# Retention and two gated layers on one core: one shared GpSimd/VectorE port in the planner, held slots for partial sums, a later sine table, and one raw weight buffer for each stream

## The chip, the cores and the metric

One core of one Trainium2 chip. The metric is device time of one execution in microseconds (us), median of several runs. Engines by the profile's names: PE (TensorE, matmul), PEld (its weight loads), DVE (VectorE), ACT (ScalarE), POOL (GpSimd), SP (SyncE, which issues the DMAs here).

## The reference

```python
# retention, per head h (B=2, H=8, S=768, D=64), float32
state = gamma * state + outer(k[t], v[t]);   y[t] = scale * q[t] @ state
x = y as (1536 tokens, 512)
# first layer pair: weights (512, 2048) and (2048, 512)
h = x @ w1_in;  x = (h * tanh(softplus(h))) @ w1_out
# second layer pair, same shapes
h = x @ w2_in;  out = (h * cos(h)) @ w2_out
```

q, k, v are float32, the four weight matrices are drawn as 64-bit floats and reach the chip as raw bits (pairs of 32-bit words).

## The kernel before, in words

**Stages.** The retention runs first (to about 44 us). Then come eight groups `gi = 4 m + G`: m is the layer pair (0 mish, 1 cosine), G one of four column groups of 512 of the 2048 inner features. Tokens lie in three blocks j of 512. A product in float32 is three matmuls of rounded halves (`TERMS`: high x high, high x low, low x high).

**First layer of a group.** For group 0 all three blocks go by `gemm1` (L552). From group 1 on, blocks 0 and 1 are done together by a scheme that needs seven products where eight would do the plain way, `wino` (L510), in two half passes p = 0, 1 of `mini` (L883). A half pass is one product of six matmuls after the other on PE: p1, p2, p6, a fill, p5, a fill, c12, p7, a fill, p4. A *fill* is one unit of second-layer work, six matmuls of `gemm2` (L580), taken from an iterator `before` with `take`. Between the products, partial sums move: ACT copies bank d to the tile U (`wino_copy`, L518) after p1, p6 and p5, and DVE adds U to a bank (`wino_add`, L521), called c11, c22 and c21. p6, p5 and c12 write the bank that a copy has just read, so each waits for its copy; p4 accumulates on the bank that c22 writes, so p4 waits for c22. Block 2 goes by `gemm1` between half passes. After each block and half, ACT takes the activation (mish, L587, or the cosine in several steps from L601), rounds it to g (L630), and DVE makes the low part of g (L634); the second layer then uses it.

**Second layer.** Eight `gemm2` units for each block of a group, in bank pairs; DVE adds the result to `acc` (`out_add`, L650).

**Weights.** A tile of weights is `(which, gi, u)`: "i" or "o" (first or second layer), u = 0, 1 one half of the group's. SP loads it in two DMAs of 512 KB (`w_load`, L240) into a raw buffer. Both streams share one ring of two raw buffers (`raw_p`, L211). DVE turns the bits into float32: `w_abs` L252, `w_clamp` L258, `w_exponent` L262, `w_sign` L268, `w_low` L289. ACT rounds the high part (L283), POOL makes the low part (L297). For "i" tiles POOL and ACT also build T, the sums and differences that the seven-product scheme needs (L306, L312, L316, L320, L324); T's raw sums lie in the raw buffer, so that of an "i" tile is held until T is done.

**What sets the order.** The program is written down as operations of a `Plan` (L86): each has an engine, a cost in us, what it needs and which buffers it uses. `order` (L139) is a list scheduler over these costs. PE's operations keep the order in which they are written; for DVE, ACT, POOL and SP the planner picks what is ready first, then what has the longest tail. In before, a shared DVE operation (`SHARED`) that would start in a POOL operation waits for its end, and the other way round, but each looks only at the last operation of the other side. The instructions are then issued in that order, and each engine runs its own in that order.

**Places that the prediction speaks of.** The first half pass, of group 1, follows 13 fill units (8 of `tiles_out(0,0,0)`, 5 by `take(before, AHEAD[0])`). The half pass of group 4 is the first of the cosine layer: `at["sin"]` is an ACT operation (L590) that loads ACT's table for the sine and may run once the last mish is done.

```python
take(before, AHEAD[0])                 # AHEAD = (5, 5)
for gi in range(1, 2 * NG):
    mini(m, G, 0, lambda: take(before, 1))
    g_split()
    take(before, AHEAD[1] if G else 3)
```

Of the kernel before, what the change touches and what calls it, by code (L numbers as in the profile page):

```python
# [61 lines left out]
AHEAD = (5, 5)  # L62

# [22 lines left out]
class Plan:  # L86
# [5 lines left out]
    AHEAD = 1000  # L92
# [11 lines left out]
    def op(self, engine, cost, fn, *args, needs=(), uses=(), new=None):  # L104
        n = len(self.ops)
        uses = list(uses)
        before = set(needs)
        reuse = []
        for key, bufs, *tag in [] if new is None else new if isinstance(new, list) else [new]:
            line = self.lines.setdefault(tag[0] if tag else key[0], [])  # L110
            if line:
                before.add(self.owner[line[-1]])
            if len(line) >= bufs:
                reuse.append(line[-bufs])
            line.append(key)
# [10 lines left out]
        self.ops.append(dict(engine=engine, cost=cost, fn=fn, args=args, before=before, reuse=reuse, att=att))  # L126
        return n

    def wait(self, n, after):
        first, then = self.ops[n]["engine"], self.ops[after]["engine"]  # L130
        if first == then or first is None:
            return 0.0
        return self.LANDING if first == "SP" else self.WIRE
# [5 lines left out]
    def order(self):  # L139
# [21 lines left out]
        pool = shared = (0.0, 0.0)  # L161
        self.start, self.end, order = {}, {}, []
        while ready:
            first = {}
# [7 lines left out]
            for e in first.keys() & {"DVE", "ACT"}:  # L172
                t, _, n = first[e]
                for k, at in ready.items():
                    at = max(at, free[e])
                    if ops[k]["engine"] == e and at < t + ops[n]["cost"] and tail[k] > tail[first[e][2]] + self.AHEAD:
                        first[e] = (at, -tail[k], k)
            t, _, n = min(first.values())
            o = ops[n]
            e = o["engine"]  # L180
            if self.shares(n):
                shared = (t, t + o["cost"])
            if e == "POOL":
                t = shared[1] if shared[0] <= t < shared[1] else t
                pool = (t, t + o["cost"])
# [18 lines left out]
def retention_two_mlps(ctx: ExitStack, tc: tile.TileContext, qkv, w1i, w1o, w2i, w2o, consts, out):  # L204
# [6 lines left out]
    raw_p = ctx.enter_context(tc.tile_pool(name="raw", bufs=2))  # L211
# [19 lines left out]

    def w_load(it, ns):
        which, gi, u = it
        m, G = divmod(gi, NG)
        src = (wins if which == "i" else wouts)[m]
        if it not in raw_t:
            raw_t[it] = raw_p.tile([128, 2, 512, 2], U32, tag="raw", name="raw")
# [90 lines left out]
    att = {}  # L328
# [347 lines left out]
    def weight(it, between=lambda: None):  # L676
        raw, mag, w = ("raw", it), ("mag", it), ("w", it)
        first, single = it == ("i", 0, 0), it[:2] in (("i", 0), ("o", 0))
        if single:
            loads = [op("SP", 1.25, w_load, it, (0,), new=(raw, 2))]  # L680
            between()
            loads.append(op("SP", 1.25, w_load, it, (1,), uses=[raw]))
        else:
            loads = [op("SP", 2.5, w_load, it, (0, 1), new=(raw, 2))]
        for load, ns in zip(loads, [slice(0, 1), slice(1, 2)] if single else [slice(0, 2)]):
# [5 lines left out]
            elif first:  # L691
                at["act", it, ns.start] = last = op("ACT", 0.62, w_abs_act, it, ns.start, needs=[load], new=new, uses=[raw, mag])
            else:
                at["act", it, ns.start] = last = op("DVE", 0.75 * c, w_abs, it, ns, needs=[load], new=new, uses=[raw, mag])
            at["clamp", it, ns.start] = last = op("DVE", 0.75 * c, w_clamp, it, ns, needs=[last], uses=[mag])
            at["exponent", it, ns.start] = last = op("DVE", 0.75 * c, w_exponent, it, ns, needs=[last], uses=[mag])
            last = op("DVE", 1.27 * c, w_sign, it, ns, needs=[last], uses=[mag, raw])
# [4 lines left out]
            def low_op(needs):  # L702
                at["dve low", it, ns.start] = n = op("DVE", 1.27 * c, w_low, it, ns, single, needs=needs, uses=[mag, raw])
                return n

            def high_op(needs):
                at["high", it, ns.start] = n = op("ACT", 1.08 * c, w_high_part, it, ns, needs=needs, uses=[mag, w])
# [10 lines left out]
            for n in range(ns.start, ns.stop):  # L718
                at["w", it, n] = op(
                    *(("DVE", 0.72) if on_dve else ("POOL", 1.25)), w_low_part, it, slice(n, n + 1), on_dve,  # L720
                    needs=[high, low], uses=[w, raw if single else mag],
                )
        if it[0] == "i" and it[1]:
            t = ("T", it)
            last = op("POOL", 1.1, w_first_differences, it, needs=[low], uses=[raw, mag])
            last = op("POOL", 0.75, w_second_sum, it, needs=[last], uses=[raw, mag])
            last = op("POOL", 0.75, w_last_difference, it, needs=[last], uses=[raw, mag])
            last = op("ACT", 1.06, w_t_high, it, needs=[last, at["ret"]], new=(t, 1, "T"), uses=[raw])
            for part in (slice(0, 2), slice(2, 4)):
                at["T", it] = op("POOL", 1.25, w_t_low, it, part, needs=[last], uses=[raw, t])  # L730
# [103 lines left out]
    def tile_in(m, G, j, f, parts=range(KD), only=None):  # L834
# [16 lines left out]
        if m == 0:  # L851
            at["g"].append((k, [op("ACT", 1.06, mish, k, needs=[last, at["table"]], uses=hs)], hs))
# [3 lines left out]
    def cosine(unit, needs, hs):  # L856
# [3 lines left out]
        last = op("ACT", 0.58 * n, cos_whole, unit, needs=needs + [at["angle"], at["sin"]], new=[(a, 1, t) for t in lines], uses=hs)  # L860
        last = op("DVE", 0.64 * n, cos_angle, unit, needs=[last], uses=[a] + hs)
        last = op("ACT", 0.58 * n, cos_size, unit, needs=[last], uses=[a])
        last = op("ACT", 0.58 * n, cos_clamp, unit, needs=[last], uses=[a])
        last = op("ACT", 0.58 * n, cos_sin, unit, needs=[last], uses=[a])
        return op("DVE", 0.64 * n, g_mul, unit, needs=[last], uses=[a] + hs)

    def g_split():

        while at["g"] and free_g:
# [4 lines left out]
            if len(needs) > 1:  # L874
                at["g", k] = []
                for f in range(2):
                    high = op("ACT", 0.62, half_high, k, f, needs=[needs[f]], new=None if f else new, uses=[g, uses[f]])
                    at["g", k].append(op("DVE", 0.72, half_low, k, f, needs=[high], uses=[g, uses[f]]))
                continue
            last = op("ACT", 1.06, g_high, k, needs=needs, new=new, uses=uses)  # L880
            at["g", k] = [op("DVE", 1.35, g_low, k, needs=[last], uses=[g] + uses)]

    def mini(m, G, p, fill):  # L883
# [31 lines left out]
        for j, (needs, hs) in enumerate((([c11, c12], [b["c"], b["d"]]), ([c21, c22], [b["b"], b["a"]]))):  # L915
            k = (gi, j, p)
            if m == 0:
                at["g"].append((k, [op("ACT", 1.06, mish, k, needs=needs + [at["table"]], uses=hs)], hs))
# [5 lines left out]
    def tile_out(m, G, j, d, u, cols=slice(0, DM)):  # L924
# [17 lines left out]
        if G == 0:  # L942
            last = op("ACT", 1.05, out_first, m, G, j, p, needs=[last, at["close"]], uses=os + [acc], new=None if p else (acc, NJ))
        else:
            last = op("DVE", 1.25, out_add, m, G, j, p, needs=[last] + prior, uses=os + [acc])
        at["acc", m, j, p] = [last]
        if m == 0 and G == NG - 1:
            x = ("x", 1, j)
            if (j, p) != (1, 0):
                high = op("ACT", 1.05, x2_high, j, p, needs=[last], uses=[acc, x], new=None if x in plan.owner else (x, 1, "x%d" % j))  # L950
                at.setdefault(x, []).append(op("DVE", 1.27, x2_low, j, p, needs=[high], uses=[acc, x]))
# [161 lines left out]
    def sums(m, needs, done):  # L1113
# [9 lines left out]
        def sum_of(to, a, b, plus, *after):  # L1123
            return op("DVE", 1.27, s_op, m, to, a, b, plus, needs=[new, *after], uses=uses)
# [5 lines left out]
        for n, last in ((3, s3), (2, s2), (1, s1), (4, s4)):  # L1130
            more = uses + ([("x", m, 1)] if n == 4 else [])
            high = op("ACT", 1.05, s_high, m, n, needs=[last, *(done if n == 4 else [])], uses=more)
            at["S", m, n] = [op("DVE", 1.27, s_low, m, n, needs=[high], uses=more)]
        return s1, s2, s3, s4

    read = sums(0, [at["ret"]], j1_done)
# [17 lines left out]
    take(before, AHEAD[0])  # L1154
    for gi in range(1, 2 * NG):
# [4 lines left out]
        take(before, AHEAD[1] if G else 3)  # L1160
# [74 lines left out]
```

## Time and profile before

| what | us |
| --- | --- |
| median of 3 runs (lowest, highest) | 558.77 (556.99, 558.89) |
| profiled execution, its own time | 560.37 |
| its span | 558.3 |
| PE busy | 547.9 (98%) |
| DVE, ACT, POOL busy | 393.2, 314.0, 189.6 |
| mean granted TensorE clock | 0.994 of full speed |

The profile is of one execution, 1.60 us above the median of the runs. Its time is 2.07 us longer than its span. PE is busy nearly all the time, so the rows to read are those that tell when PE waited.

### The profile page before, as it was taken

How to read it: one execution, taken by the hardware profiler on the slowest of the kernel's cores; microseconds unless marked ns; L12 is line 12 of the kernel's file. 1: busy time of each engine (PE TensorE's matmuls, PEld its weight loads, DVE VectorE, ACT ScalarE, POOL GpSimd, SP SyncE). 2: the span in 40 equal slices, each digit the busy share in tenths (PEclk: the TensorE clock that was granted, in tenths of full speed). 3: DMA queues.
4: the chain of work that ended last, by engine and by line, in shares of the span. 5: the costliest groups of instructions: out<-in, count | busy, mean ns of one | idle time of the engine just before them, and what ended most of it. 6: DMA issues, size and time to landing. Idle time of an engine off the chain costs nothing.

```text
span 558.3 us, 7458 instructions
## 1 busy us (share of the span) xinstructions
PE 547.9 (98%) x2968; PEld 455.2 (82%) x2968; DVE 393.2 (70%) x449; ACT 314.0 (56%) x417; POOL 189.6 (34%) x166
## 2 busy tenths in 40 slices
PE   8999999899999999999999999999999999999997
PEld 6898888688888888888877888888888888888886
DVE  5689896877365586457787798659849696768452
ACT  4374453444233314333185997899586867786360
POOL 6670007436341155114422317332541146131000
PEclk9899999999999999999998999999999999999999
DMA  8982310250222210222201220131201222020103
GB/s 290 411 328 101 127 75 1 76 209 18 75 77 75 77 56 20 75 77 76 76 0 62 89 76 15 66 146 76 77 0 77 75 76 75 1 76 1 75 22 130
DMA packets 16162, 49.33 MB, mean 88 GB/s; under 512 B 1792, under 2 KB 2176, under 8 KB 16128
## 3 DMA queue, kind: packets, MB, share of 16 engines
q1 hardware_dynamic: 16128, 48.86, 23.5%
q8 instruction: 23, 0.38, 0.3%
q14 instruction: 11, 0.09, 0.0%
HBM read 45.71 MB, written 3.15 MB: 87 GB/s over the span
## 4 chain that ended last, share of the span: by engine, by line
PE 94%; DMA 2%; DVE 1%; ACT 1%; issue 1%; POOL 0%; SPq 0%; DVEq 0%
PE bank L580 46%; PE bank L510 23%; PE bank L552 20%; DMA qkv<-qkv_dram 2%; PE bank L436 2%; PE bank L397 1%; PE bank L446 1%; PE bank L411 1%; DVE mag L262 0%; DVE bank L521 0%; POOL raw L306 0%; ACT L590 0%; DVE mag L289 0%; DVE mag L268 0%; DVE mag L258 0%
## 5 line engine op out<-in xcount | busy, mean ns | idle before, releaser
L580 PE MATMUL bank<-g,wo 128*128 128x512 f32 x576 | 137.2, 392 | 0.0
L580 PE MATMUL bank<-wo,g 128*128 128x512 f32 (+2 forms) x588 | 136.1, 385 | 0.0
L580 PEld LDWEIGHTS bank<-g,wo 128*128 128x128 f32 x576 | 109.0, 189 | 22.8
L580 PEld LDWEIGHTS bank<-wo,g 128*128 128x128 f32 x588 | 109.1, 188 | 22.4 <-POOL wo L297 0.4
L552 PE MATMUL bank<-x,wi 128*128 128x512 f32 x480 | 110.2, 389 | 0.0
L552 PEld LDWEIGHTS bank<-x,wi 128*128 128x128 f32 x480 | 90.0, 188 | 18.8 <-issue 0.2
L324 POOL TENSOR_TENSOR T<-raw,T 128x512 fp32r<-128x512 f32 x28 | 39.0, 1412 | 92.3 <-ACT T L320 78.7
L297 POOL TENSOR_TENSOR wo<-mag,wo 128x512 fp32r<-128x512 f32 x28 | 36.6, 1328 | 93.9 <-ACT wo L283 82.5
L634 DVE TENSOR_TENSOR g<-bank,g 128x1024 fp32r<-128x1024 f32 x40 | 48.8, 1221 | 26.8 <-ACT g L630 26.7
L510 PE MATMUL bank<-S,T 128*128 128x512 f32 x252 | 64.8, 392 | 2.4 <-ACT U L518 2.4
L510 PE MATMUL bank<-x,wi 128*128 128x512 f32 x252 | 61.8, 389 | 0.0
L650 DVE TENSOR_TENSOR acc<-bank,acc 128x1024 f32<-128x1024 f32 x35 | 42.8, 1222 | 25.6 <-PE bank L580 25.2
L510 PEld LDWEIGHTS bank<-S,T 128*128 128x128 f32 x252 | 47.4, 189 | 13.1 <-ACT U L518 3.3
L521 DVE TENSOR_TENSOR bank<-bank,U 128x512 f32<-128x512 f32 x42 | 29.3, 697 | 38.1 <-PE bank L510 37.2
L623 DVE TENSOR_TENSOR bank<-angle,bank 128x512 f32<-128x512 f32 (+1 forms) x32 | 30.6, 959 | 36.0 <-ACT angle L619 35.8
L510 PEld LDWEIGHTS bank<-x,wi 128*128 128x128 f32 x252 | 47.2, 188 | 10.0 <-ACT U L518 0.2
L587 ACT ACTIVATE bank<-bank 128x1024 f32<-128x1024 f32 x24 | 24.2, 1009 | 53.1 <-PE bank L552 37.3
L518 ACT COPY U<-bank 128x512 f32<-128x512 f32 x42 | 24.6, 586 | 50.5 <-PE bank L510 50.0
L297 POOL TENSOR_TENSOR wi<-mag,wi 128x512 fp32r<-128x512 f32 x28 | 40.4, 1464 | 33.3 <-ACT wi L283 33.3
L306 POOL TENSOR_TENSOR raw<-mag 128x512 f32<-128x512 f32 x14 | 19.2, 1372 | 91.8 <-DVE mag L289 62.5
L630 ACT CAST g<-bank 128x1024 fp32r<-128x1024 f32 x40 | 40.7, 1017 | 8.5 <-DVE bank L623 5.2
L268 DVE SCALAR_TENSOR_TENSOR mag<-raw,mag 128x1024 uint32<-128x1024 uint32 (+1 forms) x36 | 43.0, 1196 | 0.6
(82 smaller groups left out, 628.6 us busy)
## 6 DMA issues: line engine op xcount, KB each, us to landing
raw<-w1i_dram SPq DMA_DIRECT2D x16, 512.0 KB, 4.0
raw<-w1o_dram SPq DMA_DIRECT2D x16, 512.0 KB, 4.0
raw<-w2i_dram SPq DMA_DIRECT2D x16, 512.0 KB, 3.6
raw<-w2o_dram SPq DMA_DIRECT2D x16, 512.0 KB, 3.7
qkv<-qkv_dram SPq DMA_DIRECT2D x12, 512.0 KB, 7.4
qkv<-qkv_dram SPq DMA_DIRECT2D x22, 256.0 KB, 6.9
out_dram<-acc SPq DMA_DIRECT2D x11, 256.0 KB, 2.0
out_dram<-acc SPq DMA_DIRECT2D x1, 160.0 KB, 1.7
```

The costliest lines, as they stand in the source:

```text
L268: nc.vector.scalar_tensor_tensor(out=a, in0=high, scalar=0xC0000000, in1=a, op0=ALU.bitwise_and, op1=ALU.bitwise_or)
L297: eng.tensor_sub(out=w[:, :, 1], in0=w_all_of(it, single)[:, ns].bitcast(F32), in1=w[:, :, 0].bitcast(F32))
L324: nc.gpsimd.tensor_sub(out=t[:, :, 1], in0=t_of(it)[:, part], in1=t[:, :, 0].bitcast(F32))
L510: nc.tensor.matmul(ps, lhs, rhs, start=(not more and kk + i == 0), stop=(kk == 1 and i == last), skip_group_check=True)
L518: nc.scalar.copy(out=copies[0][:, n], in_=bank[:, WINO_BANK["d"], :])
L521: nc.vector.tensor_add(out=bank[:, WINO_BANK[to], :], in0=bank[:, WINO_BANK[of], :], in1=copies[0][:, n])
L552: nc.tensor.matmul(h, w[:, f % 2, a, kk * 128 : (kk + 1) * 128], x[:, b, kk, :], start=(a + b + kk == 0), stop=(a == 1 and kk == KD - 1),)
L580: nc.tensor.matmul(ps, lhs, rhs, start=(n == 0), stop=(n == 3 * GF - 1))
L623: nc.vector.tensor_mul(out=h, in0=a, in1=h)
L630: nc.scalar.copy(out=g_t[k][:, :, 0, :], in_=h_of(k))
L634: nc.vector.tensor_sub(out=g[:, :, 1, :], in0=h_of(k), in1=g[:, :, 0, :].bitcast(F32))
L650: nc.vector.tensor_add(out=acc, in0=o_of((m * NG + G, j, p)), in1=acc)
```

## The change

Six things, in the words of the code. **1.** `FIRST = 8`: eight units and not five are taken before the first half pass. **2.** In the half pass p = 0 of group 4 the sine table is held until after the first copy, and one more fill unit stands between p2 and p6; 4 units and not 3 are taken behind it (and in that place of every group with G = 0, which is group 4 alone). **3.** The planner keeps one time `port` that POOL operations and shared DVE operations take in turns; "due" operations (`wino_copy`, and the `wino_add` that is c22) have their engine kept clear when they come up within 0.4 us; another rule picks a longer tail on DVE and ACT; most costs, waits and overlaps are set anew. **4.** `HEAD`: the new waits and rules hold from the sums on, the retention keeps the old ones. **5.** The ring of two raw buffers becomes two buffers with a name each: from group 1 on "o" tiles use `raw0` and "i" tiles `raw1` (`("i", 1, 0)` uses `raw0`). **6.** A product counts as a user of T only if it reads T.

```diff
+FIRST = 8
 class Plan:
-    AHEAD = 1000
+    OVERLAP = {"DVE": 0.09, "ACT": 0.1, "POOL": 0.04}
+    DUE = (("wino_copy",), ("wino_add", "a"))
+    SLACK = 0.4
+    NEAR, MORE = 0.5, 2.0
...
     def order(self):
...
-                if self.shares(n) and pool[0] <= t < pool[1]:
-                    t = pool[1]
+                if e == "POOL" or self.shares(n):
+                    t = max(t, port)
+                if e in due and not ops[n]["due"] and t < due[e] + self.SLACK < t + ops[n]["cost"]:
+                    t = max(t, due[e])
...
+                    if f != n and t < first[e][0] + self.NEAR * ops[f]["cost"] and tail[n] > tail[f] + self.MORE:
+                        first[e] = (t, -tail[n], n)
...
+            if e == "POOL" or self.shares(n):
+                port = end
             if e:
-                free[e] = end
+                free[e] = end - (self.OVERLAP.get(e, 0.0) if n >= self.HEAD else 0.0)
...
-    raw_p = ctx.enter_context(tc.tile_pool(name="raw", bufs=2))
+    raw_p = ctx.enter_context(tc.tile_pool(name="raw", bufs=1))
...
+    def raw_slot(it):
+        which, gi, u = it
+        if gi == 0 or it == ("i", 1, 0):
+            return "raw%d" % u
+        return "raw%d" % (which == "i")
...
-            loads = [op("SP", 2.5, w_load, it, (0, 1), new=(raw, 2))]
+            loads = [op("SP", 2.5, w_load, it, (0, 1), new=(raw, 1, raw_slot(it)))]
...
-            uses = [b[to], ("w", it), ("T", it), ("x", m, 0), ("x", m, 1), ("S", m)]
+            uses = [b[to], ("w", it), ("x", m, 0), ("x", m, 1), ("S", m)] + [("T", it)] * (w[0] == "T")
...
         copy1 = copy(0, p1)
+        if gi == NG and p == 0:
+            hold(at["sin"], copy1)
         p2 = pe(1)
+        if gi == NG and p == 0:
+            fill()
...
-    take(before, AHEAD[0])
+    take(before, FIRST)
...
-        take(before, AHEAD[1] if G else 3)
+        take(before, AHEAD[1] if G else 4)
```

No engine gets more or fewer instructions. Line numbers in the changed kernel are 21 higher from the middle on (L510 is L531, L580 is L601, L518 is L539).

**PE at the first half pass** (gemm1 of group 0, then fill units, then the seven products). Before:

```order
L552 MATMUL bank<-x,wi 128x512 x144
L580 MATMUL bank<-g,wo 128x512 x78
L510 MATMUL bank<-x,wi 128x512 x12
L510 MATMUL bank<-S,T 128x512 x6
L580 MATMUL bank<-g,wo 128x512 x6
```

Now:

```order
L573 MATMUL bank<-x,wi 128x512 x144
L601 MATMUL bank<-g,wo 128x512 x96
L531 MATMUL bank<-x,wi 128x512 x12
L531 MATMUL bank<-S,T 128x512 x6
L601 MATMUL bank<-g,wo 128x512 x6
```

16 units of six stand ahead of p1 where 13 stood.

**ACT at the first half pass of group 4** (L587 and L608 are the last mish, L630 and L651 the rounding of its g, L590 and L611 the table load and the small activation that asks for it, L601 and L622 the first step of a cosine). Before:

```order
L587 ACTIVATE bank<-bank 128x1024
L630 CAST g<-bank 128x2x512
L590 ACT_TABLE_LOAD
L590 ACTIVATE spare<-quarter 128x1
L283 CAST wi<-mag 128x2x512
L518 COPY U<-bank 128x512
L601 ACTIVATE angle<-bank 128x512
L518 COPY U<-bank 128x512
```

Now:

```order
L608 ACTIVATE bank<-bank 128x1024
L539 COPY U<-bank 128x512
L651 CAST g<-bank 128x2x512
L611 ACT_TABLE_LOAD
L611 ACTIVATE spare<-quarter 128x1
L622 ACTIVATE angle<-bank 128x512
L304 CAST wi<-mag 128x2x512
L539 COPY U<-bank 128x512
```

The first copy moves ahead of g, the table and the weights' high part.

**DVE at the first half pass of group 2** (L268, L289 are the sign and low part of an "o" tile, L521 the adds c11, c22 and c21, L650 `out_add`). Before:

```order
L268 SCALAR_TENSOR_TENSOR mag<-raw,mag 128x1024
L289 SCALAR_TENSOR_TENSOR mag<-raw,mag 128x1024
L521 TENSOR_TENSOR bank<-bank,U 128x512
L650 TENSOR_TENSOR acc<-bank,acc 128x1024
L521 TENSOR_TENSOR bank<-bank,U 128x512
L634 TENSOR_TENSOR g<-bank,g 128x2x512
```

Now:

```order
L289 SCALAR_TENSOR_TENSOR mag<-raw,mag 128x1024
L542 TENSOR_TENSOR bank<-bank,U 128x512
L310 SCALAR_TENSOR_TENSOR mag<-raw,mag 128x1024
L671 TENSOR_TENSOR acc<-bank,acc 128x1024
L273 TENSOR_SCALAR mag<-raw 128x1024
L279 TENSOR_SCALAR mag<-mag 128x1024
L542 TENSOR_TENSOR bank<-bank,U 128x512
```

c11 now comes ahead of the low part (L310), and the first two steps of the next "o" tile (L273, L279) stand between `out_add` and c22.

## Rows read from the trace of the kernel before

**Rows 1.** The page: busy time of each engine, share of the span, instructions.

```profile
PE   547.9 (98%) x2968; PEld 455.2 (82%) x2968; DVE 393.2 (70%) x449; ACT 314.0 (56%) x417; POOL 189.6 (34%) x166
```

**Rows 2.** PE's waits from 44 us on: line <- releaser: total us, times, longest.

```profile
PE bank L510 <- ACT U L518: 2.4, 1, 2.4
PE bank L510 <- DVE bank L521: 2.2, 1, 2.2
```

**Rows 3.** Chain that ended last, half passes of group 1: start, us, what.

```profile
94.78 2.73 PE bank L510 x12
...
109.33 1.66 PE bank L510 x6
110.99 6.80 PE bank L580 x30
117.79 4.08 PE bank L510 x18
...
131.39 10.88 PE bank L580 x48
```

**Rows 4.** Timeline of DVE, 102 to 110 us: start, us, line, operation, tiles.

```profile
102.91 0.69 DVE L252 TENSOR_SCALAR mag<-raw 128x1024 uint32<-128x1024 uint32 x1 [2.22 <-POOL raw L312]
103.64 1.11 DVE L258 TENSOR_SCALAR mag<-mag 128x1024 f32<-128x1024 f32 x1
104.78 1.66 DVE L262 TENSOR_SCALAR mag<-mag 128x1024 uint32<-128x1024 uint32 x1
106.48 2.19 DVE L268 SCALAR_TENSOR_TENSOR mag<-raw,mag 128x1024 uint32<-128x1024 uint32 x1
108.59 0.69 DVE L521 TENSOR_TENSOR bank<-bank,U 128x512 f32<-128x512 f32 x1
```

**Rows 5.** Timeline of POOL beside it.

```profile
104.16 3.42 POOL L297 TENSOR_TENSOR wi<-mag,wi 128x512 fp32r<-128x512 f32 x2
```

**Rows 6.** Chain that ended last, first half pass of group 4.

```profile
278.52 10.89 PE bank L552 x48
...
294.47 1.91 PE bank L510 x6
...
307.27 4.08 PE bank L580 x18
```

**Rows 7.** Timeline of ACT, 289 to 295 us.

```profile
289.43 1.01 ACT L587 ACTIVATE bank<-bank 128x1024 f32<-128x1024 f32 x1 [1.06 <-PE bank L552]
290.47 1.01 ACT L630 CAST g<-bank 128x1024 fp32r<-128x1024 f32 x1
291.51 1.28 ACT L590 ACT_TABLE_LOAD   x1
292.80 0.20 ACT L590 ACTIVATE spare<-quarter 128x1 f32<-128x1 f32 x1
292.91 1.03 ACT L283 CAST wi<-mag 128x1024 fp32r<-128x1024 f32 x1
293.85 0.58 ACT L518 COPY U<-bank 128x512 f32<-128x512 f32 x1
```

**Rows 8.** Busy time by stretch (length, PE, PEld, DVE, ACT, POOL), granted clock PEclk, DMA.

```profile
292.00:294.00 2.00, 0.12 (x1) 0.00 (x0) 1.88 (x2) 1.99 (x4) 0.00 (x0) 1.00 0.00 0
296.00:298.00 2.00, 2.00 (x6) 1.52 (x6) 2.00 (x3) 1.54 (x3) 1.52 (x1) 0.50 0.00 0
```

**Rows 9.** Line L240 (raw weight loads) from 90 us on.

```profile
L240 SPq DMA_DIRECT2D raw<-w2o_dram x16: 327/380/434, 268.8 to 488.1; - x16
DMA to landing us min/median/max: 3.1/4.0/5.5
```

**Rows 10.** The same line over the whole trace.

```profile
DMA to landing us min/median/max: 3.0/4.0/8.0
```

**Rows 11.** Group of DVE's low part of a weight tile, by shape: busy, mean ns of one.

```profile
L289 DVE SCALAR_TENSOR_TENSOR mag<-raw,mag 128x1024 uint32<-128x1024 uint32 x28 | 38.4, 1372 | 0.6
```

**Rows 12.** Chain that ended last: p1, p2 and p6 of group 2's first half pass.

```profile
159.95 4.19 PE bank L510 x18
```

More of the change, by code (lines that the diff above doesn't have):

```diff
@@ L160, in order @@
         free = {o["engine"]: 2.6 if o["engine"] == "SP" else 0.0 for o in ops}
-        pool = shared = (0.0, 0.0)
+        port = 0.0
         self.start, self.end, order = {}, {}, []
         while ready:
-            first = {}
+            first, due = {}, {}
+            for n, t in ready.items():
+                if ops[n]["due"]:
+                    e = ops[n]["engine"]
+                    due[e] = min(due.get(e, t), t)
             for n, t in ready.items():
@@ L679, in weight @@
         if single:
-            loads = [op("SP", 1.25, w_load, it, (0,), new=(raw, 2))]
+            loads = [op("SP", 1.25, w_load, it, (0,), new=(raw, 1, raw_slot(it)))]
             between()
@@ L693, in weight @@
             else:
[L694 to L697, printed above, removed]
+                at["act", it, ns.start] = last = op("DVE", 0.69 * c, w_abs, it, ns, needs=[load], new=new, uses=[raw, mag])
+            at["clamp", it, ns.start] = last = op("DVE", 0.69 * c, w_clamp, it, ns, needs=[last], uses=[mag])
+            at["exponent", it, ns.start] = last = op("DVE", 0.69 * c, w_exponent, it, ns, needs=[last], uses=[mag])
+            last = op("DVE", 1.22 * c, w_sign, it, ns, needs=[last], uses=[mag, raw])
             if not ns.start:
@@ L702, in low_op @@
             def low_op(needs):
-                at["dve low", it, ns.start] = n = op("DVE", 1.27 * c, w_low, it, ns, single, needs=needs, uses=[mag, raw])
+                at["dve low", it, ns.start] = n = op("DVE", 1.22 * c, w_low, it, ns, single, needs=needs, uses=[mag, raw])
                 return n
             def high_op(needs):
-                at["high", it, ns.start] = n = op("ACT", 1.08 * c, w_high_part, it, ns, needs=needs, uses=[mag, w])
+                at["high", it, ns.start] = n = op("ACT", 1.05 * c, w_high_part, it, ns, needs=needs, uses=[mag, w])
                 return n
@@ L724, in weight @@
             t = ("T", it)
[L725 to L728, printed above, removed]
+            last = op("POOL", 1.27, w_first_differences, it, needs=[low], uses=[raw, mag])
+            last = op("POOL", 0.74, w_second_sum, it, needs=[last], uses=[raw, mag])
+            last = op("POOL", 0.74, w_last_difference, it, needs=[last], uses=[raw, mag])
+            last = op("ACT", 1.05, w_t_high, it, needs=[last, at["ret"]], new=(t, 1, "T"), uses=[raw])
             for part in (slice(0, 2), slice(2, 4)):
-                at["T", it] = op("POOL", 1.25, w_t_low, it, part, needs=[last], uses=[raw, t])
+                at["T", it] = op("POOL", 1.29, w_t_low, it, part, needs=[last], uses=[raw, t])
                 last = at["T", it]
@@ L851, in tile_in @@
         if m == 0:
-            at["g"].append((k, [op("ACT", 1.06, mish, k, needs=[last, at["table"]], uses=hs)], hs))
+            at["g"].append((k, [op("ACT", 1.01, mish, k, needs=[last, at["table"]], uses=hs)], hs))
         else:
@@ L917, in mini @@
             if m == 0:
-                at["g"].append((k, [op("ACT", 1.06, mish, k, needs=needs + [at["table"]], uses=hs)], hs))
+                at["g"].append((k, [op("ACT", 1.01, mish, k, needs=needs + [at["table"]], uses=hs)], hs))
             elif j:
@@ L942, in tile_out @@
         if G == 0:
-            last = op("ACT", 1.05, out_first, m, G, j, p, needs=[last, at["close"]], uses=os + [acc], new=None if p else (acc, NJ))
+            last = op("ACT", 1.02, out_first, m, G, j, p, needs=[last, at["close"]], uses=os + [acc], new=None if p else (acc, NJ))
         else:
-            last = op("DVE", 1.25, out_add, m, G, j, p, needs=[last] + prior, uses=os + [acc])
+            last = op("DVE", 1.22, out_add, m, G, j, p, needs=[last] + prior, uses=os + [acc])
         at["acc", m, j, p] = [last]
@@ L1123, in sum_of @@
         def sum_of(to, a, b, plus, *after):
-            return op("DVE", 1.27, s_op, m, to, a, b, plus, needs=[new, *after], uses=uses)
+            return op("DVE", 1.22, s_op, m, to, a, b, plus, needs=[new, *after], uses=uses)
         s3 = sum_of(3, (0, 0), (1, 0), False)
```

56 lines of the change are left out of this document (28 added, 28 removed).

## The prediction

> **What bounds the kernel now.** I read the page first: PE is busy for 547.9 us of a span of 558.3 [rows 1], and the change gives no engine an instruction more or less. So the work of PE is a floor, and what can be won is the 10.4 us in which PE has nothing to do, and any time in which it works at a lower clock. The second view is the list of PE's waits, where the reader is to see how short it is [rows 2]: behind the retention there are two single waits, 2.4 us for an ACT copy and 2.2 us for a DVE add, both in half passes. The other 10.4 - 4.6 = 5.8 us lie in the retention, whose order the change leaves alone, and behind the last matmul. All other waits of DVE, ACT, POOL and SP are covered by PE. The third view is the chain that ended last, to price both places with what surrounds them.
>
> An undisturbed half pass is ten blocks of six matmuls. Group 1's second one shows it: it begins at 117.79 and its last product ends at 131.39 [rows 3], so 13.60 us, 1.36 for a block. On that scale, counted from the start of p1: p1 ends at 1.36, p2 at 2.72, p6 at 4.08, then fill 5.44, p5 6.80, fill 8.16, c12 9.52, p7 10.88, fill 12.24, p4 13.60.
>
> **First place: c22 in the first half pass.** It begins at 94.78 and p4 ends at 110.99 [rows 3]: 16.21 us, a loss of 16.21 - 13.60 = 2.61. The DVE timeline shows why [rows 4]. c22 could run once p7 has ended, at 94.78 + 10.88 = 105.66; but DVE is in the conversion of a weight tile, and in its order w_clamp (1.11), w_exponent (1.66) and w_sign (2.19) come first. c22 ends only at 109.28. These three are long because POOL makes the low part of another tile at the same time [rows 5]; where POOL is idle, w_abs takes 0.69 [rows 4].
>
> Part 1 of the change puts three more units ahead, 3 x 1.36 = 4.08 us. p1 begins at 94.78 + 4.08 = 98.86, p7 ends at 109.74, and c22 must be done at 98.86 + 12.24 = 111.10. The DVE work ahead of c22 does not hang on PE's half pass, save for c11 (0.69). Even if it gets no faster, it ends with w_sign at 106.48 + 2.19 = 108.67, or 109.36 with c11 added to it. c22 then runs from 109.74 to 110.43, with 0.7 us to spare. **Term: -2.61.** The three units are taken from the same list, so the second half pass now fills with units of its own group, and needs their "o" tile at its first fill, 98.86 + 13.60 + 6.80 + 4.08 = 123.34. That tile's w_low ends behind c22 at 110.43 + 1.37 = 111.8 [rows 11], its two low parts on POOL 3.42 later [rows 5], at 115.2, or 118.6 if another tile's two go first. I cost this at nothing; if those 5 us of cover were gone, each us of lateness would be a us.
>
> **Second place: the sine table in group 4.** p1 starts at 278.52 + 10.89 = 289.41, p4 ends at 307.27 [rows 6]: 17.86 us, a loss of 4.26. ACT finishes the last mish at 290.44, p1 ends at 290.77, but the copy that p6 waits for starts at 293.85: ahead of it stand the rounding of g (1.01), the table load (1.28), its small activation (0.20) and a weight's high part (1.03) [rows 7]. PE waits 2.4 of the 4.26 [rows 2]. The rest is clock: PE is almost idle from 292 to 294, and from 296 to 298 it runs at a granted 0.50, the 1.2 GHz level [rows 8]; 4.26 - 2.36 = 1.90 us go there. (2.36 is the same wait with one more digit: the copy frees p6 at 294.47, and p2 would have ended at 292.13.)
>
> Part 2 puts the copy right behind the mish: 290.77 to 291.35. p2 ends at 292.13 and the added fill at 293.49, so p6 finds its copy done. Behind the copy ACT has g 1.01, table 1.48, a first cosine step of about 0.6 (an estimate from the copy of the same shape, 0.58) and the high part 1.03, in all 4.1: until 295.5. The second copy needs p6, which ends at 294.85, so it runs to about 296.1; p5 wants it when the next fill ends, at 296.21. That is close, 0.1 us and a little more by the overlap of neighbouring ACT rows, but a miss costs tenths only. No idle PE means no fall of the clock. The added fill is a unit that stood behind the half pass, so it costs nothing itself. One more unit is taken behind, so the second half pass fills with units of the cosine layer, some 25 us after the mish; they need g of its block 0 and the "o" tile, whose steps are the same as above, and I estimate 1 to 3 us of cover. **Term: -4.26.**
>
> **The planner.** Its new costs and the shared port only change the order on ACT, DVE, POOL and SP, all with cover under PE. What it can win there is small: two half passes in which a high part stands ahead of the first copy take 4.19 and not 4.08 for their first 18 matmuls (group 2's [rows 12], and group 3's likewise), 0.22 in all. What it can lose: it no longer lets DVE's conversions run beside POOL, so conversions start later but are shorter. The bounds are a gain of 0.22 and, from the nearest row, one c22 late by one stretched operation, 2.19 [rows 4], at one place. I take 0, since due operations are kept clear and every place that I walked has some tenths left, and keep both ends.
>
> **One raw buffer for each stream.** This adds a wait: the next "o" load can start only when w_low has read the tile before it. The sharpest place is the first half pass of group 2. DVE's order there is c11, w_low, out_add, w_abs, w_clamp, c22. c11 runs to 2.72 + 0.70 = 3.42, w_low (mean 1.37 [rows 11]) to 4.8. The load's second DMA is issued about 0.43 later and lands after 3.1 to 5.5, median 4.0 [rows 9]: at 9.2 in the median. w_abs and w_clamp (0.69 each, w_clamp taken like w_abs) then end at 10.6, before p7's end at 10.88: nothing lost. At 5.5 they end at 12.1, c22 at 12.8, 0.57 us late. **Term: 0**, up to +0.6.
>
> The Trainium skill ("Trainium Kernel Development and Optimization", section Best Practices) says to double-buffer for performance, so that DMA overlaps compute. It speaks against this part: with one buffer the load of a stream stands in series with its conversion. By the rule the sum would lose what the last rival below says; by the rows the median load has 0.3 us left.
>
> **Sum.** -2.61 - 4.26 = -6.87. The profiled execution goes from 560.37 to 553.5, its span from 558.3 to 551.4. The profiled execution is 1.60 above the median of the runs, so the median goes from 558.77 to **551.9**.
>
> **Rivals.** (A) is the forecast, with a range of its own from 550.2 (0.22 of the copies, and the 1.8 us by which the lowest run lies under the median, most of it) to 553.0 (one late c22 or load, or some misses of tenths). Chance 0.74.
>
> (B) One of the two waits stays, or one of its size takes its place. If c22 of the first half pass is still late, only the sine place is won: 558.77 - 4.26 = 554.5. If the copy in group 4 is again behind the table, only the first: 558.77 - 2.61 = 556.2. For it: the margins are 0.1 to 0.7 us. Against: a miss costs the overshoot, not the whole wait, unless the clock falls as well. Chance 0.12; 0.10 of it for 554.5 and times below 556.0, 0.02 for 556.2.
>
> (C) The change does not do what it says: the places are mended, but waits of the same size come up at other half passes because the planner's picture of the shared port is off, and DVE, ACT and POOL have other stretches than it thinks. About 558.8. Against: in 12 of the 14 half passes PE has no wait now [rows 2]. Chance 0.08.
>
> (D) It gets slower by the one-buffer "o" stream. DVE runs in its order, so a load that is late holds w_abs, and c22 behind it. The point from which this decides is a landing later than 12.24 - 0.70 - 1.38 - 0.43 - 4.8 = 4.9 us. The longest landing of the trace is 8.0 [rows 10]; then w_clamp ends at 14.6, c22 at 15.3, 3.1 us late, and with the clock falling as in group 4 another 1.9: 5.0 at a place. Two such places are 10.0 - 6.87 = +3.1: 561.9. For it: there are half a dozen places of this kind. Against: the 8.0 was in the retention, when other loads ran; from 90 us on the longest is 5.5 [rows 9]. Chance 0.06.
>
> **How the numbers follow.** 0.5% is 2.8 us, about what a measurement can tell from no change. Faster by more, below 556.0: A and 0.10 of B, 0.84. Within: C and 0.02 of B, 0.10. Slower: D, 0.06. The range takes A with its own ends and B to its far end, 550.2 to 556.2; C, D and what lies under 550.2 are left out, under 2 in 10.
>
> **What would show it.** In the profile of the changed kernel: PE's waits without a line for the copies or the adds, or only tenths; p1 of the first half pass some 4.1 us later and both half passes 13.6 us (group 4: 15.0 with its added fill); granted clock 1.00 from 290 to 310 us; PE's busy time about 546, as the stretch at the lower clock is gone. Wrong would be a wait of PE for an add that itself waited for w_abs and a load (D), or a copy behind the table (B), or a new line in the waits at groups 2 to 7 (C).

## The result and the profile after

The changed kernel takes 552.54 us (median of 4 runs, 551.24 to 554.14), the kernel before 558.83 (4 runs): a ratio of 0.9895, 95% interval 0.9857 to 0.9932, so 1.1% faster. The profiled execution took 553.33 us, with a span of 551.6.

The page and PE's waits of the changed kernel (line <- releaser: total, times, longest):

```profile
PE   544.9 (99%) x2968; PEld 454.0 (82%) x2968; DVE 393.4 (71%) x449; ACT 313.8 (57%) x417; POOL 183.8 (33%) x166
```

```profile
PE bank L432 <- DMA qkv<-qkv_dram: 2.1, 1, 2.1
PE bank L1032 <- DVE back_turn L1038: 1.1, 1, 1.1
PE bank L457 <- issue: 0.6, 1, 0.6
```

All three lie in the retention. Both waits of [rows 2] are gone and none has come in their place. The chain that ended last answers to [rows 3] and [rows 6]:

```profile
77.78 21.76 PE bank L601 x96
99.54 4.08 PE bank L531 x18
...
113.14 6.80 PE bank L601 x30
...
287.22 2.72 PE bank L531 x12
289.94 1.36 PE bank L601 x6
...
302.18 5.44 PE bank L601 x24
```

The first half pass takes 113.14 - 99.54 = 13.60 us, where it took 16.21. That of group 4, which now has one block more in it, takes 302.18 - 287.22 = 14.96 = 11 x 1.36, where it took 17.86 for ten. So both run at the pace of an undisturbed one.

The retention differs between executions by more than either of these (the first matmul of group 0 starts between 41.9 and 44.9 us in the profiled executions of this study; 44.16 before, 44.85 after). So I compare stretches by PE's timeline: from the start of one group's `gemm1` block to the next one's ("group 1" runs from group 0's block to group 1's), and "behind" for the whole from the first one to the end of the span, all behind the retention. Each is read from the one profiled execution of a kernel; "the rest" lies between 223.67 and 223.84 in the ten kernels in which PE has no wait there, so a difference of 0.2 in "behind" tells little.

| us | group 1 | groups 2, 3 | group 4 | the rest | behind |
| --- | --- | --- | --- | --- | --- |
| before | 97.95 | 136.24 | 56.27 | 223.68 | 514.14 |
| changed | 95.33 | 136.00 | 51.74 | 223.68 | 506.75 |
| difference | -2.62 | -0.24 | -4.53 | 0.00 | -7.39 |

The span gained less, 6.7, as this execution's retention took 0.69 longer. The 0.24 in groups 2 and 3 are the two first copies that stood behind a weight's high part, the 0.22 that the prediction gave as the planner's best.

### The profile page after: what moved, and what is told of

Read it like the earlier page. It is cut to its first block, busy times and chain, and to the rows that moved or that the text cites. A ratio compares the mean times of both kernels' runs of the same rounds, so it can differ in the third digit from the quotient of the medians.

```text
span 551.6 us, 7436 instructions
## 1 busy us (share of the span) xinstructions
PE 544.9 (99%) x2968; PEld 454.0 (82%) x2968; DVE 393.4 (71%) x449; ACT 313.8 (57%) x417; POOL 183.8 (33%) x166
## 3 DMA queue, kind: packets, MB, share of 16 engines
HBM read 45.71 MB, written 3.15 MB: 89 GB/s over the span
## 4 chain that ended last, share of the span: by engine, by line
PE 97%; DMA 2%; issue 0%; SPq 0%; DVE 0%
PE bank L601 47%; PE bank L531 24%; PE bank L573 20%; DMA qkv<-qkv_dram 2%; PE bank L457 2%; PE bank L418 1%; PE bank L432 1%; PE bank L467 1%; SPq L997 0%; DVE acc L678 0%
## 5 line engine op out<-in xcount | busy, mean ns | idle before, releaser
L601 PE MATMUL bank<-wo,g 128*128 128x512 f32 (+2 forms) x588 | 136.1, 385 | 0.0
L601 PE MATMUL bank<-g,wo 128*128 128x512 f32 x576 | 135.8, 389 | 0.0
L601 PEld LDWEIGHTS bank<-wo,g 128*128 128x128 f32 x588 | 109.0, 188 | 22.2 <-DVE g L551 0.2
L601 PEld LDWEIGHTS bank<-g,wo 128*128 128x128 f32 x576 | 108.1, 188 | 22.5
L531 PE MATMUL bank<-S,T 128*128 128x512 f32 x252 | 64.0, 389 | 0.0
L531 PE MATMUL bank<-x,wi 128*128 128x512 f32 x252 | 61.7, 389 | 0.0
L531 PEld LDWEIGHTS bank<-S,T 128*128 128x128 f32 x252 | 47.3, 188 | 9.8
L531 PEld LDWEIGHTS bank<-x,wi 128*128 128x128 f32 x252 | 47.3, 188 | 9.8
L608 ACT ACTIVATE bank<-bank 128x1024 f32<-128x1024 f32 x24 | 24.2, 1008 | 54.5 <-PE bank L573 39.0
L345 POOL TENSOR_TENSOR T<-raw,T 128x512 fp32r<-128x512 f32 x28 | 37.4, 1353 | 45.1 <-ACT T L341 45.1
L539 ACT COPY U<-bank 128x512 f32<-128x512 f32 x42 | 24.6, 586 | 39.8 <-PE bank L531 39.6
L651 ACT CAST g<-bank 128x1024 fp32r<-128x1024 f32 x40 | 40.6, 1016 | 11.5 <-DVE bank L644 7.5
L626 DVE SCALAR_TENSOR_TENSOR angle<-bank,angle 128x512 f32<-128x512 f32 (+1 forms) x32 | 30.5, 954 | 22.2 <-ACT angle L622 22.1
```

Source lines behind the costliest of these rows:

```text
L345: nc.gpsimd.tensor_sub(out=t[:, :, 1], in0=t_of(it)[:, part], in1=t[:, :, 0].bitcast(F32))
L531: nc.tensor.matmul(ps, lhs, rhs, start=(not more and kk + i == 0), stop=(kk == 1 and i == last), skip_group_check=True)
L539: nc.scalar.copy(out=copies[0][:, n], in_=bank[:, WINO_BANK["d"], :])
L601: nc.tensor.matmul(ps, lhs, rhs, start=(n == 0), stop=(n == 3 * GF - 1))
L626: nc.vector.scalar_tensor_tensor(out=a, in0=h, scalar=INV_2PI, in1=a.bitcast(I32), op0=ALU.mult, op1=ALU.subtract)
L651: nc.scalar.copy(out=g_t[k][:, :, 0, :], in_=h_of(k))
```

## The experiments

Two theories stood against each other. **P**, that of the prediction: the two edits of the written order (eight units first; the sine table) earn the gain, and the planner nothing. **Q**: the planner's order earns it by itself. Each stretch is measured as in the table above; the times are medians of several runs, with the ratio to the kernel before of the same chip.

### The edits under the old planner

```diff
-    take(before, AHEAD[0])
+    take(before, 8)
```

> The kernel before with part 1 alone: eight units ahead of the first half pass, old planner, old ring. Theory P (the two edits of the written order earn the gain, the planner nothing): c22 of the first half pass loses its wait, 2.61 us less than before; but the old planner now also puts w_low of the same tile (1.23 to 2.19) ahead of c22, which by the durations of before ends c22 at 111.3 to 112.2 where 111.10 is wanted, so a wait of 0.2 to 1.1 stays and the gain is 1.5 to 2.4. The copy in group 4 still waits 2.4 us. Theory Q (the planner's order earns the gain by itself, the edits are not needed): part 1 alone moves little, under 1 us, as DVE's order ahead of c22 is the old one.

556.60 us, ratio 0.9960 (0.9939 to 0.9981). Group 1 takes 95.33, as in the changed kernel: -2.62. DVE did have w_low ahead of c22 as well, yet had finished it at 109.18 and waited 0.84 for PE: in this order POOL's two low parts run from 102.38 to 105.38, beside w_abs and w_clamp (1.76 and 1.67), and w_exponent, w_sign and w_low meet none of POOL's work (0.69, 1.23 and 1.23). Group 4 is untouched, 56.23, and of the waits of [rows 2] the 2.4 us for the copy is left.

P for group 1, and more than I had expected of it.

```diff
         copy1 = copy(0, p1)
+        if gi == NG and p == 0:
+            hold(at["sin"], copy1)
         p2 = pe(1)
+        if gi == NG and p == 0:
+            fill()
...
-        take(before, AHEAD[1] if G else 3)
+        take(before, AHEAD[1] if G else 4)
```

> The kernel before with part 2 alone: the sine table held behind the first copy, one fill more between p2 and p6, 4 units behind. Theory P: the copy is done at about 292.9 where p6 comes at 293.49, so no wait and no lower clock in group 4, 4.26 us less than before; c22 of the first half pass still waits 2.2. Theory Q: the old planner has g and a weight's high part ahead of the copy in this order too, so a wait of about 1 us stays and the gain is 2 us or less.

558.82 us, ratio 0.9999 (0.9983 to 1.0016): nothing. P missed. Q has the gain right (2 us or less) and the order (g and a high part ahead of the copy), but not the wait: the first copy is done in time now. Behind the retention the kernel takes 513.93, only 0.21 less. Beside c22's wait in group 1 (2.0), which this run leaves in, these waits of PE stand in place of the one of 2.4:

```profile
PE bank L510 <- ACT U L518: 1.2, 2, 0.8
...
PE bank L580 <- DVE g L530: 0.9, 2, 0.6
PE bank L552 <- DVE g L634: 0.5, 1, 0.5
```

Group 4 won 0.88 and the groups behind it lost 0.80. The run with both edits shows the same with group 1 mended:

> The kernel before with parts 1 and 2, old planner, old ring. Theory P: nearly the whole gain, 5.8 to 6.9 us, as in the changed kernel. Theory Q: about half of it or less, under 4 us, with waits left at both places.

555.97 us, ratio 0.9956 (0.9943 to 0.9970); behind the retention 511.51, -2.63. That is the gain of the first edit alone. Its timelines of DVE, ACT and PE in group 4 show the first copy (287.48) and how the first two of the new waits come about:

```profile
287.82 2.22 DVE L498 TENSOR_TENSOR x<-acc,x 128x1024 fp32r<-128x1024 f32 x1
289.96 0.69 DVE L521 TENSOR_TENSOR bank<-bank,U 128x512 f32<-128x512 f32 x1
```

```profile
285.63 1.02 ACT L630 CAST g<-bank 128x1024 fp32r<-128x1024 f32 x1
286.54 1.05 ACT L283 CAST wi<-mag 128x1024 fp32r<-128x1024 f32 x1
287.48 0.59 ACT L518 COPY U<-bank 128x512 f32<-128x512 f32 x1
...
290.68 0.60 ACT L601 ACTIVATE angle<-bank 128x512 int32<-128x512 f32 x1 [1.09 <-DVE bank L521]
291.18 0.58 ACT L518 COPY U<-bank 128x512 f32<-128x512 f32 x1
```

```profile
291.81 1.66 PE L510 MATMUL bank<-S,T 128*128 128x512 f32 x6 [0.46 <-ACT U L518]
293.30 1.54 PE L580 MATMUL bank<-g,wo 128*128 128x512 f32 x6
295.58 1.66 PE L510 MATMUL bank<-x,wi 128*128 128x512 f32 x6 [0.74 <-ACT U L518]
```

DVE's low part of x (L498) runs beside POOL and takes 2.22, where the same step on the tile S has a median of 1.22; c11 is late behind it, the cosine's first step waits for c11, and the second copy, which PE needs at 291.81, stands behind that step; the third, needed at 295.58, stands behind three more cosine steps. The table was one obstacle; the order behind it had the next ones ready. P falls for part 2, and its planner term with it.

### The planner without the edits

```diff
-    take(before, FIRST)
+    take(before, AHEAD[0])
...
-        if gi == NG and p == 0:
-            hold(at["sin"], copy1)
...
-        if gi == NG and p == 0:
-            fill()
...
-        take(before, AHEAD[1] if G else 4)
+        take(before, AHEAD[1] if G else 3)
```

> The changed kernel without parts 1 and 2 (five units first, no hold, no added fill, three units behind): planner, one raw buffer for each stream and T's users alone. Theory P: the time of before within 1 us, both waits there. Theory Q: c22 stands ahead of w_exponent and the copy ahead of g in this order, so both waits are gone without the edits and the gain is 6 to 7 us.

552.19 us, ratio 0.9882 (0.9859 to 0.9905): by the medians not to be told from the changed kernel. Behind the retention 508.11, -6.03 of the -7.39. **Q holds for most of the gain.** ("Planner alone" is parts 3 to 6 of the change. Part 6 moves no instruction: with the old users of T the program comes out the same. Part 5 is tried below.) Group 1 takes 95.55 with five units only, since c22 stands ahead of w_exponent (L283) now; group 4 takes 52.87, since the copy stands ahead of g and the table without any hold. The timelines of DVE and of ACT:

```profile
103.35 1.11 DVE L279 TENSOR_SCALAR mag<-mag 128x1024 f32<-128x1024 f32 x1
104.39 0.69 DVE L542 TENSOR_TENSOR bank<-bank,U 128x512 f32<-128x512 f32 x1
...
106.12 0.68 DVE L283 TENSOR_SCALAR mag<-mag 128x1024 uint32<-128x1024 uint32 x1
```

```profile
286.38 0.59 ACT L539 COPY U<-bank 128x512 f32<-128x512 f32 x1 [0.35 <-PE bank L531]
286.86 1.02 ACT L651 CAST g<-bank 128x1024 fp32r<-128x1024 f32 x1
287.90 1.28 ACT L611 ACT_TABLE_LOAD   x1
```

What the edits add is 0.22 in group 1 and 1.13 in group 4, where PE waits 0.6 for the low part of an "o" tile (and is busy 0.52 longer):

```profile
PE bank L601 <- POOL wo L318: 0.6, 2, 0.3
```

Taking part 2 alone out of the changed kernel (the last three places of the diff above, with FIRST left in) says which edit that is:

> The changed kernel without part 2 (no hold, no added fill, three units behind); part 1 and the planner stay. From the planner alone, group 1 was 0.2 and group 4 1.1 longer than in the changed kernel. Theory: part 1 brings the 0.2 in group 1, and the 1.1 in group 4 stays (PE waits for POOL's low part of an o tile, as with the planner alone), so 1.1 behind the retention. Rival: the 1.1 was a matter of the load order that part 1 changes too; then group 4 is as in the changed kernel.

552.96 us, ratio 0.9885 (0.9847 to 0.9922); group 1 95.38, group 4 53.18, with 0.8 us of the same wait; behind 508.22. So part 2 is worth some 1.4 us under the new planner, by the added fill and the unit behind. The hold itself is worth nothing there: with only that line left out, the instructions and their order come out the same.

### Which part of the planner

The port taken out of the planner without the edits:

```diff
-            if e == "POOL" or self.shares(n):
-                port = end
```

> Planner alone (as in the run without parts 1 and 2), and of the planner the shared port taken out: POOL and shared DVE operations may be planned side by side. Theory Q1 (the shared port is what moves c22 of the first half pass): its order has w_exponent, w_sign and w_low ahead of c22 again, so group 1 is some 2.4 us or more longer than in the run with the port, with PE waiting for a DVE add there; group 4 stays as it was, as the copy still stands ahead of g. Theory Q2 (the costs or the due rule do it): group 1 stays within 0.5 us of that run.

562.24 us, ratio 1.0056 (1.0026 to 1.0086): slower than before. Behind 515.78, 7.67 more than with the port. Group 1 is 1.75 longer, less than expected, and not by c22 (DVE had finished at 104.65, PE did not wait) but by a copy behind a weight's high part in the second half pass; most of the loss lies in the cosine layer. PE's waits, and DVE and POOL at the longest one:

```profile
PE bank L529 <- DVE bank L540: 4.0, 3, 2.3
PE bank L529 <- ACT U L537: 2.1, 3, 1.2
```

```profile
358.13 1.65 DVE L287 SCALAR_TENSOR_TENSOR mag<-raw,mag 128x1024 uint32<-128x1024 uint32 x1
359.81 2.20 DVE L308 SCALAR_TENSOR_TENSOR mag<-raw,mag 128x1024 uint32<-128x1024 uint32 x1
361.93 0.68 DVE L624 SCALAR_TENSOR_TENSOR angle<-bank,angle 128x512 f32<-128x512 f32 x1
362.53 0.68 DVE L540 TENSOR_TENSOR bank<-bank,U 128x512 f32<-128x512 f32 x1
```

```profile
358.65 4.49 POOL L316 TENSOR_TENSOR wi<-mag,wi 128x512 fp32r<-128x512 f32 x2
```

The mechanism of [rows 4, 5] again, at another place: DVE's sign and low part beside POOL's two low parts, and c22 behind them. Q1 is right that the new planner's gain hangs on the port, and wrong that it does so at the first half pass. The run leaves the planner no picture of the port at all, where the kernel before had a partial one; so it does not tell what one shared time is worth over two halves.

The cost figures of before, first without the edits (two of 29 lines, without their indents):

```diff
-at["act", it, ns.start] = last = op("DVE", 0.69 * c, w_abs, it, ns, needs=[load], new=new, uses=[raw, mag])
+at["act", it, ns.start] = last = op("DVE", 0.75 * c, w_abs, it, ns, needs=[load], new=new, uses=[raw, mag])
...
-last = op("ACT", 0.2 + 0.43 * n, cos_size, unit, needs=[last], uses=[a])
+last = op("ACT", 0.58 * n, cos_size, unit, needs=[last], uses=[a])
```

> Planner alone, with the cost figures of before and all of the new rules. Theory Q3 (the new costs are what moves the copy of group 4): its order has g and the table ahead of the copy again, though no longer the weight's high part, so the copy starts about 0.9 earlier than in before: PE waits 1.4 in group 4, and with the clock group 4 is 2.5 to 3.5 us longer than in the run with new costs; group 1 stays mended (c22 ahead of w_clamp). Theory Q4 (the rules do it, costs are nothing): group 4 within 0.5 us.

554.58 us, ratio 0.9936 (0.9906 to 0.9966); group 1 95.34, group 4 54.91. PE waited 1.42 for the copy, as Q3 says, with the table ahead of it:

```profile
286.70 1.28 ACT L611 ACT_TABLE_LOAD   x1
...
288.10 0.57 ACT L539 COPY U<-bank 128x512 f32<-128x512 f32 x1
```

Group 4 is 2.04 longer than with new costs, not 2.5 to 3.5: the granted clock stayed at 1.00 (287 to 297 us).

The same cost figures in the changed kernel with its edits:

> The changed kernel with the cost figures of before, all rules and edits in. Its order has g and a high part ahead of the first copy of group 4, but the table behind it, so the copy is done about 3.5 us after p1's start where p6 comes at 4.08. Theory: with the rules and the edits the old costs lose nothing there; 0 to 1.1 us behind the retention, the 1.1 if POOL's low part is late again. Rival (costs carry the gain): 2 us or more.

551.64 us, ratio 0.9851 (0.9829 to 0.9873). Group 4 51.79, behind 506.92: PE has no wait behind the retention. So with the new rules and the edits, the old costs do.

The other way round, the kernel before with both edits and the new figures (the diff above reversed):

> The kernel before with parts 1 and 2 and the new cost figures, but the old rules (two halves of a port, old waits, one ring). With old costs it gave back in groups 4 and 5 all that the sine edit won: these two were 118.8 us where the changed kernel has 114.3. Theory S (the exclusive port is needed): 2 us or more of the 4.5 remain, with PE waiting for DVE or a copy behind stretched DVE work. Theory C (only the cost figures of the cosine steps were off): under 1 us remains.

554.43 us, ratio 0.9902 (0.9884 to 0.9920); behind 510.18. Groups 4 and 5 take 117.45, 3.15 of the 4.5 remain: by theory S's number, new costs do not replace the rules. Which of the rules is missing, the port or another, this run does not tell. PE waits

```profile
PE bank L580 <- DVE g L530: 1.6, 2, 0.9
PE bank L510 <- DVE bank L521: 0.7, 1, 0.7
```

the first line behind DVE work that the old rules had put beside POOL (x's low part again, L666, 1.82); the add of the second line (c22) stands behind w_sign and w_low at 1.23 each, with POOL idle.

Last, the due rule taken out of the changed kernel:

```diff
-    DUE = (("wino_copy",), ("wino_add", "a"))
+    DUE = ()
```

> The changed kernel with no due operations (copies and c22 are kept clear by nothing but their tail). Its order differs in few places. Theory: the shared port and the costs carry the gain; behind the retention within 0.5 us of the changed kernel. Rival: the due rule carries it; waits for copies or adds come back, 1 us or more.

550.89 us, ratio 0.9839 (0.9820 to 0.9857); behind 506.79, no wait. The due rule earns nothing here. In its profiled execution the retention was shorter, with group 0 from 41.91 on; what comes behind takes the changed kernel's time.

### The single raw buffer

```diff
-    raw_p = ctx.enter_context(tc.tile_pool(name="raw", bufs=1))
+    raw_p = ctx.enter_context(tc.tile_pool(name="raw", bufs=2))
...
-            raw_t[it] = raw_p.tile([128, 2, 512, 2], U32, tag=raw_slot(it), name="raw")
+            raw_t[it] = raw_p.tile([128, 2, 512, 2], U32, tag="raw", name="raw")
...
-            loads = [op("SP", 2.5, w_load, it, (0, 1), new=(raw, 1, raw_slot(it)))]
+            loads = [op("SP", 2.5, w_load, it, (0, 1), new=(raw, 2))]
```

> The changed kernel with the ring of two raw buffers of before in place of one buffer for each stream. The prediction's step (term 0): no wait of PE in either, the time behind the retention within 0.5 us of the changed kernel. Theory R (the split earns part of the gain, as a load no longer waits for the other stream's conversion): some waits of PE for adds or low parts, 1 us or more longer.

551.94 us, ratio 0.9880 (0.9815 to 0.9945); behind 506.87 against 506.75, no wait of PE in either. The split earns nothing and costs nothing.

```diff
             nc.sync.dma_start(out=to, in_=of)
+            if which == "o" and gi > 0:
+                nc.sync.dma_start(out=to, in_=of)
```

> The changed kernel, with both DMAs of every o tile from group 1 on issued twice, into the same place: each landing is later by the second copy, estimated 2.6 to 3.1 us from 512 KB at the 334 to 411 GB/s of this trace's busiest stretches, and 0.8 of issue. The prediction's point for rival D is a landing later than 4.9 us; here they come at about 7. Theory D: in group 2's first half pass w_abs starts at about 170, c22 ends at 172.2 where 170.26 is wanted, so 1.9 us of waiting there and likewise at some of the first half passes behind, 4 to 10 us in all. If the one buffer has far more cover than I worked out: under 1 us.

601.76 us, ratio 1.0774 (1.0712 to 1.0836), far more than the 4 to 10 us that I expected. The delay was mis-sized: the second DMA into the same place is issued only after the first has landed, 3.26 us later (4.13 for the tile's other half), so in group 2 the tile came 11.0 us after its first issue and not 7. SP, DVE and PE there:

```profile
168.46 0.33 SPq L261 DMA_DIRECT2D raw<-w1o_dram  x1
171.72 0.33 SPq L263 DMA_DIRECT2D raw<-w1o_dram  x1
```

```profile
179.47 0.69 DVE L275 TENSOR_SCALAR mag<-raw 128x1024 uint32<-128x1024 uint32 x1 [8.99 <-DMA raw<-w1o_dram]
180.20 0.70 DVE L281 TENSOR_SCALAR mag<-mag 128x1024 f32<-128x1024 f32 x1
180.81 0.69 DVE L544 TENSOR_TENSOR bank<-bank,U 128x512 f32<-128x512 f32 x1
```

```profile
181.56 2.92 PE L533 MATMUL bank<-x,T 128*128 128x512 f32 x6 [5.54 <-DVE bank L544]
```

The mechanism of rival D is there, step by step. In the changed kernel the tile comes 4.72 after its first issue, 6.3 earlier, and PE does not wait; here it waits 5.54. The first issue comes 4.7 us after p1's start in both, so the cover is 6.29 - 5.54 = 0.75 us.

## Why the prediction was right, and where it was not

Forecast 551.9, measured 552.54; profiled 553.5 against 553.33, span 551.4 against 551.6. **The number is right; the account of who earns it is not.**

- **First half pass, -2.61:** group 1 is 2.62 shorter, p1 starts at 99.54 (forecast 98.86; the retention was 0.69 longer). DVE's timeline of the changed kernel, the answer to [rows 4]:

```profile
106.66 1.22 DVE L289 SCALAR_TENSOR_TENSOR mag<-raw,mag 128x1024 uint32<-128x1024 uint32 x1
110.53 0.70 DVE L542 TENSOR_TENSOR bank<-bank,U 128x512 f32<-128x512 f32 x1 [2.65 <-PE bank L531]
```

w_sign ends at 107.88, and c22 starts as p7 has ended. Part 1 earns this by itself under the old planner; but the new planner earns 2.40 of it without part 1.

- **Sine table, -4.26:** group 4 is 4.53 shorter. ACT and the clock, the answers to [rows 7] and [rows 8]:

```profile
287.26 1.01 ACT L608 ACTIVATE bank<-bank 128x1024 f32<-128x1024 f32 x1 [0.67 <-PE bank L573]
288.62 0.59 ACT L539 COPY U<-bank 128x512 f32<-128x512 f32 x1 [0.35 <-PE bank L531]
289.10 1.02 ACT L651 CAST g<-bank 128x1024 fp32r<-128x1024 f32 x1
290.14 1.28 ACT L611 ACT_TABLE_LOAD   x1
...
292.97 0.58 ACT L539 COPY U<-bank 128x512 f32<-128x512 f32 x1
```

```profile
292.00:294.00 2.00, 2.00 (x10) 1.65 (x10) 2.00 (x3) 1.91 (x4) 0.85 (x1) 1.00 0.00 0
...
296.00:298.00 2.00, 2.00 (x11) 1.65 (x10) 1.97 (x4) 0.85 (x2) 0.15 (x1) 1.00 0.00 0
```

The copies and the clock came as forecast. **The step that failed** is "Part 2 puts the copy right behind the mish ... Term: -4.26". Under the old planner part 2 moves the table, but g and a high part stay ahead of the copy; the first copy holds PE no longer, yet later copies and low parts do, and part 2 wins 0.2 in all. Under the new one the copy goes right behind the mish with no hold.

- **The planner, "I take 0":** the second failed step, and the same error seen from the other side. Without the edits it is worth 6.03, and with them 511.51 - 506.75 = 4.76. I had read the order of the whole changed kernel, in which planner and edits are one, and booked what I saw there to the edits. The sum came out right because I priced the two places in the order of the whole, whoever cures them; that the terms fit says nothing of their causes.

Behind the retention, all runs side by side (us against before's 514.14):

| | no edits | both edits |
| --- | --- | --- |
| old rules, old costs | 0 | -2.63 |
| old rules, new costs | not tried | -3.96 |
| new rules, old costs | -4.05 | -7.22 |
| new rules, new costs | -6.03 | -7.39 |
| the same, port taken out | +1.64 | not tried |

The new rules with the edits do nearly all. Beside the new rules, the costs are worth 1.98 without the edits and 0.17, within the scatter, with them; beside the old rules and the edits, 1.33. Which of the other new rules (waits, overlap, longer tails) is needed beside the port stays open, as does the port's share with the edits in and what one shared time is worth over the old two halves.

- **One raw buffer, term 0:** right. In group 2 I put the tile at 9.2 and w_clamp's end at 10.6 after p1; counted from 158.02 the rows give 9.4 and 10.83:

```profile
167.42 0.69 DVE L273 TENSOR_SCALAR mag<-raw 128x1024 uint32<-128x1024 uint32 x1 [2.70 <-DMA raw<-w1o_dram]
168.15 0.70 DVE L279 TENSOR_SCALAR mag<-mag 128x1024 f32<-128x1024 f32 x1
169.01 0.70 DVE L542 TENSOR_TENSOR bank<-bank,U 128x512 f32<-128x512 f32 x1 [0.16 <-PE bank L531]
```

The advice to double-buffer, in the Trainium skill ("Trainium Kernel Development and Optimization", section Best Practices), bought nothing here: two buffers shared by both streams and one for each take the same time as long as the loads land as here (at most 5.1 from 90 us on in the changed kernel, 5.5 in [rows 9]). No run gave each stream two. Where loads land later, a load in series with its conversion does cost, as the doubled loads show.

- **Rival C** spoke of the planner's picture of the port being off. That fits the kernel before: the sine edit's gain was given back behind low parts of x that its order ran beside POOL (2.22 at 287.82 us and 2.33 at 319.40 in the run with both edits). That the picture of the port alone did it is not shown.
- **PE's busy time** fell to 544.9, below the 546 forecast: behind the retention it is 2.83 less (0.42 in group 1, 0.24 in groups 2 and 3, 2.17 in group 4), of which I had 1.90 for the clock. The 0.42 went with the wait of 2.20, at a clock of 1.00 all along: a wait costs PE some tenths beyond its row. The first six matmuls behind a wait show 1.66 busy where others show 1.52 (1.66 [rows 3] is such a block), which is part of it. So the 1.90 was most likely some tenths too much for the clock alone; no run parts the two.

## What to carry to other kernels

Where a list scheduler sets the order, compare the planned orders with each part of a change left out before booking a term to a part: two parts may cure the same place, and one part alone may move the wait to the next operation in the queue. On an engine that runs in its order, an operation that takes much longer than planned (2.20 us for 1.22) delays everything behind it, so the planner must know which operations stretch each other; leaving that out cost the new planner 7.67 us here, where both hand-placed edits won 2.63 under the old one. Compare single stretches of the trace where another part of the program varies by more than the effect.

## What the runs showed that I had not expected

A wait of PE of 2.26 us (the port taken out, at 363 us) left the granted clock at 1.00, as that of 2.20 in the kernel before did; one of 2.36 and one of 5.54 were followed by 0.50, the 1.2 GHz level. And a DMA into a place that an earlier one still writes was issued only when that one had landed, 3.26 us later (SP waited for it); a tile loaded twice came 6.3 us later, where I had estimated the bare transfer, 2.6 to 3.1.

The shared port itself was not removed by planning: in the changed kernel w_clamp still takes 1.70 beside POOL at 154.49 us and 1.77 at 124.33, and DVE's busy time is 393.4 us, 393.2 before; the shorter conversions that I spoke of did not come in the sum. What changed is which operations meet there, and that copies and adds do not stand behind them.
